# A fused recurrence and maxout layer: the start-up reordered, and one more block of input taken through the transposing DMA

## The chip, the cores and the metric

The kernel runs on one core of one Trainium2 chip. The metric is the device time in microseconds (us) of one execution; a time is quoted as the median of several executions, and the single ones are given where they scatter. The profile of a kernel is one of its executions, and its span is some 2 us shorter than the device time, because it runs only from the first to the last instruction.

The engines are called as the profile calls them: PE (matrix products), PEld (loading of PE's weights, which overlaps PE), DVE (vector work), ACT (activations), POOL and SP. In this kernel POOL does almost nothing but issue the DMAs that cast fp32 to bf16, and SP almost nothing but issue the other DMAs. All of them share the core's 16 DMA engines.

## The reference

A gated linear recurrence over 4 sequences of 6144 tokens with 256 features each, and a two-layer network on its result:

```python
sig = 1.0 / (1.0 + np.exp(-f_logit))
f = lower_bound + (1.0 - lower_bound) * sig
for t in range(S):                       # h: (B, D)
    h = f[:, t] * h + (1.0 - f[:, t]) * x[:, t]
    y[:, t] = h
# y: (24576, 256), w1 and w2: (256, 1024), w_out: (1024, 256)
g = np.maximum(y @ w1, y @ w2)
out = g @ w_out                          # (24576, 256) fp32
```

The kernel uses max(a, b) = a + relu(b - a). It needs only one first-layer product, with `wd` = w2 - w1, and adds `y @ w13`, with `w13` = w1 @ w_out, to the second layer.

## The kernel before: the parts that matter

Tokens are handled in blocks of 512. The first four blocks are chunks of their own; after them a chunk is 1024 tokens, two blocks. So "chunk 4" is blocks 4 and 5, "chunk 5" blocks 6 and 7, "chunk 6" blocks 8 and 9. For the recurrence, features must lie on the partitions and tokens along the free axis, so f and x must be transposed. There are two ways to do it:

```python
    def by_xbar(c, s):
        return c >= (4, 4)[s]            # chunks 0 to 3: PE transposes; from 4 on: DMA
    NSCR = 2
    scratch = [[dram.tile([CH, D], BF16, ...) for q in range(NSCR)] for s in range(2)]

    def fetch(c):                        # issued by POOL
        for s in range(2):               # s = 0: f, s = 1: x
            ...
            elif by_xbar(c, s):
                scr = scratch[s][uses[s] % NSCR]
                uses[s] += 1
                nc.gpsimd.dma_start(     # cast fp32 -> bf16, DRAM -> DRAM
                    out=scr[0:nt, :].rearrange("(p i) d -> p (i d)", p=P), in_=...)
                held[c, s] = scr
            else:
                ...                      # cast fp32 -> bf16, DRAM -> SBUF

    def cross(c):                        # issued by SP
        for s in range(2):
            if by_xbar(c, s):
                dst = inpool.tile([P, KC, CH], BF16, name=("fT", "xT")[s])
                nc.sync.dma_start_transpose(out=dst[:, :, 0:nt], in_=held[c, s][0:nt, :])
                held[c, s] = dst
```

There are two scratch buffers for f and two for x. The cast of a chunk into a scratch buffer must therefore wait until the transposing DMA of the chunk that used it last has read it. This wait follows from `uses[s] % NSCR`.

Per block: ACT makes u = sigmoid(-f) (`gate`), DVE makes v = u * x, the decay ff = 1 + nom * u, and the scan y. PE runs the first layer (`dT`), ACT evicts it through a relu (`rt`), PE runs the second layer of the block before (`psO`), DVE evicts that (`osb`) and SP issues its store. The main loop, cut:

```python
    LEAD_FETCH = 7
    LEAD_CROSS = 3
    ...                                  # blocks 0, 1, 2; weights; w13
        for j in range(2, NBLK + 1):
            ahead("cross", cross, j + LEAD_CROSS)
            ahead("fetch", fetch, j + LEAD_FETCH)
            ...
            if j == 2:
                for fc in range(FC):
                    second_layer(1, fc)
            for fc in range(FC):
                if j < NBLK:
                    first_layer(j, fc)
                if j > 2:
                    second_layer(j - 1, fc)
                ...
                if fc == 0 and j + 1 < NBLK:
                    scans = scan_steps(j + 1)
                if fc < len(scans):
                    scans[fc]()
```

Of the kernel before, what the change touches and what calls it, by code (L numbers as in the profile page):

```python
# [9 lines left out]
FP32 = mybir.dt.float32  # L10
BF16 = mybir.dt.bfloat16
# [7 lines left out]
def kernel(  # L19
# [36 lines left out]
    def by_xbar(c, s):  # L56
        return c >= (4, 4)[s]
# [33 lines left out]
    def fetch(c):  # L91
        b, t0, nt, _ = chunks[c]
        for s in range(2):
            src = srcs[s][b, t0 : t0 + nt, :]
            if c == 0:
                raw = const.tile([P, nt // P, D], FP32, name=("f0", "x0")[s])
                nc.sync.dma_start(  # L97
                    out=raw[:], in_=src.rearrange("(p i) d -> p i d", p=P)
                )
                nat = natpool.tile([P, CH // P, D], BF16, name=("fn", "xn")[s])  # L100
                nc.vector.tensor_copy(out=nat[:, 0 : nt // P, :], in_=raw[:])  # L101
                held[c, s] = nat
            elif by_xbar(c, s):
                scr = scratch[s][uses[s] % NSCR]
                uses[s] += 1
                nc.gpsimd.dma_start(  # L106
                    out=scr[0:nt, :].rearrange("(p i) d -> p (i d)", p=P),
                    in_=src.rearrange("(p i) d -> p (i d)", p=P),
                )
                held[c, s] = scr  # L110
            else:
                nat = natpool.tile([P, CH // P, D], BF16, name=("fn", "xn")[s])
                nc.gpsimd.dma_start(
                    out=nat[:, 0 : nt // P, :].rearrange(
                        "p (k i) d -> p k (i d)", i=TB // P
                    ),
                    in_=src.rearrange(
                        "(k p i) d -> p k (i d)", p=P, i=TB // P
                    ),
                )  # L120
                held[c, s] = nat

# [38 lines left out]
    def gate(j):  # L161
        nb = blocks[j][2]
        u = midpool.tile([P, KC, TB], BF16, name="u")
        src = turned[j, 0]
        nc.scalar.activation(  # L165
            out=like(u[:, :, 0:nb], src), in_=src, func=AF.Sigmoid, scale=-1.0
        )
        us[j] = u

    def like(t, src):  # L170
        if len(src.shape) == 3:
            return t
        return t.rearrange("p k (m i) -> p k m i", m=P)

    def scan_steps(j):
# [17 lines left out]
        def drive():  # L193
            src = turned[j, 1]
            nc.vector.tensor_tensor(  # L195
                out=like(v[:, :, 0:nb], src),
                in0=like(u[:, :, 0:nb], src),
                in1=src,
                op=ALU.mult,
            )  # L200

        def scan(h):
# [15 lines left out]
            drive,  # L218
            lambda: decay(0),
            lambda: decay(1),  # L220
            lambda: scan(0),
            lambda: scan(1),
        ]

# [42 lines left out]
    def pair(w, k):  # L267
        return w[:, :, 2 * k * P : 2 * k * P + 2 * P].rearrange(
            "p kc (q m) -> p kc q m", q=2
        )  # L270

    def make_wd(k):
        g, r = divmod(k, NQ // 2)
        qs = slice(2 * r, 2 * r + 2)
        nc.vector.tensor_tensor(  # L275
            out=pair(wdf, k), in0=half(w2n, g)[:, :, qs], in1=half(w1n, g)[:, :, qs],
            op=ALU.subtract,
        )
        cols = slice(2 * k * P, 2 * k * P + 2 * P)
        for kc in range(KC):  # L280
            nc.scalar.mul(wd[:, kc, cols], wdf[:, kc, cols], om[:, kc : kc + 1])  # L281
# [101 lines left out]
    with tc.manual_schedule():  # L383
# [6 lines left out]
        fetch(0)  # L390
        for g in range(NG):
            fetch_w(g)
        nc.scalar.activation(out=warm[:], in_=om[:, 0:1], func=AF.Sigmoid)
        wt = ps_d.tile([P, TB], BF16, name="dT")
        for q in range(8):
            nc.tensor.transpose(wt[:, 0:P], ident[:], ident[:])
        turn(turn_steps(0))
        recurrence(0)
        pool_waits(w1n[0][:, 0, 0:1])
        nc.gpsimd.dma_start(  # L400
            out=wob[:].rearrange("p (g q) c -> p g (q c)", g=NG),
            in_=moe_w_out.rearrange("(g p q) c -> p g (q c)", g=NG, q=NQ),
        )
        pool_waits(w2n[1][:, 0, 0:1])
        fetch(1)
        fetch(2)
        done["fetch"] = 3
        ahead("fetch", fetch, LEAD_FETCH)
        pts = [turn_w1(0), turn_w1(1)]
        make_wd(0)  # L410
        make_wd(1)
        for fc in range(0, 2):
            first_layer(0, fc)
        keep_w1T(0, pts[0])
        make_wd(2)
        for fc in range(2, 4):
            first_layer(0, fc)
        make_wd(3)
        keep_w1T(1, pts[1])
        pts = [turn_w1(2), turn_w1(3)]  # L420
        for fc in range(4, 6):
            first_layer(0, fc)
        keep_w1T(2, pts[0])
        for fc in range(6, 8):
            first_layer(0, fc)
        keep_w1T(3, pts[1])
        make_w13()
        turn(turn_steps(1))
        recurrence(1)
        for fc in range(FC):  # L430
            second_layer(0, fc)
# [6 lines left out]
        turn(turn_steps(3))  # L438
        gate(3)
        for j in range(2, NBLK + 1):  # L440
# [9 lines left out]
            if j == 2:  # L450
                for fc in range(FC):
                    second_layer(1, fc)
            for fc in range(FC):
# [8 lines left out]
                if fc == 0 and j + 1 < NBLK:  # L462
                    scans = scan_steps(j + 1)
# [32 lines left out]
```

## Time and profile before

| | before |
|---|---|
| time, median (3 executions) | 403.2 us (403.06 to 403.27) |
| span of the profile, granted PE clock | 401.1 us, 1.000 |
| PE busy | 386.0 us, 96% |
| first first-layer matmul | 13.47 us |
| first layer of block 3 starts in full | 41.48 us |
| from there, one block | 7.82 us |

The page of the kernel before, first and fourth part (busy us, share of the span, number of instructions; then the chain of work that ended last, by engine and by line):

```profile
PE 386.0 (96%) x2744; PEld 295.1 (74%) x2792; DVE 247.5 (62%) x349; ACT 269.5 (67%) x446; POOL 27.6 (7%) x59
...
PE 94%; DVE 3%; DMA 1%; issue 1%; SPq 0%; ACT 0%; DVEq 0%
```

A block's first layer starts "in full" with the second of the two matrix products that add up to its first piece; in block 3 the first of them ran at 40.31, on the half of y that was ready.

PE is the limit, and it is used nearly without a gap. The chain, in order of time, shows the last place where anything but PE is in it (start, length, what; all in us):

```profile
33.95 2.74 PE psO L346 x25
36.71 0.69 DVE osb L366
37.41 1.12 DVE v L195
38.53 0.53 DVE ff L184 x2
39.06 2.38 DVE y L208 x2
41.48 0.38 PE dT L317
```

Block 3's first layer at 41.48 waits for DVE, which did block 3's v, ff and scans only after two evictions. After it the chain is PE alone. What is to be won lies before 41.48.

The other thing to look at is DMA traffic. SP's DMA issues in the kernel before (start and length of the issuing instruction; when SP is long at a transposing DMA, the DMA engines are slow to take it):

```profile
28.83 8.36 SPq L128 DMA_TRANSPOSE fT<-scr_0_90  x1
37.30 3.05 SPq L128 DMA_TRANSPOSE xT<-scr_0_92  x1
40.44 0.53 SPq L369 DMA_DIRECT2D out_dram<-osb  x1
41.06 2.77 SPq L128 DMA_TRANSPOSE fT<-scr_1_91  x1
```

And POOL's cast issues (in brackets POOL's wait before them, and what ended it):

```profile
17.63 0.49 POOL L106 DMA_DIRECT2D scr_1_91<-in_f_logit_dram  x1 [0.73 <-DMA fn<-in_f_logit_dram]
18.87 0.49 POOL L106 DMA_DIRECT2D scr_1_93<-in_x_dram  x1 [0.75 <-DMA xn<-in_x_dram]
41.38 0.49 POOL L106 DMA_DIRECT2D scr_0_90<-in_f_logit_dram  x1 [22.02 <-DMA fT<-scr_0_90]
42.94 0.49 POOL L106 DMA_DIRECT2D scr_0_92<-in_x_dram  x1 [1.07 <-DMA xT<-scr_0_92]
```

The casts of chunks 4 and 5 are all issued by 18.87, with no wait for a transposing DMA, since both scratch buffers are fresh; counted from the trace, their last packet starts at 31.6 us and ends at 35.8. Chunk 4's transposing DMAs (blocks 4 and 5) are issued at 28.83 and 37.30 and have the DMA engines nearly to themselves from 36 to 42 us. The next casts come only at 41.38 and 42.94, when those have landed.

### The profile page before, as it was taken

How to read it: one execution, taken by the hardware profiler on the slowest of the kernel's cores; microseconds unless marked ns; L12 is line 12 of the kernel's file. 1: busy time of each engine (PE TensorE's matmuls, PEld its weight loads, DVE VectorE, ACT ScalarE, POOL GpSimd, SP SyncE). 2: the span in 40 equal slices, each digit the busy share in tenths (PEclk: the TensorE clock that was granted, in tenths of full speed). 3: DMA queues.
4: the chain of work that ended last, by engine and by line, in shares of the span. 5: the costliest groups of instructions: out<-in, count | busy, mean ns of one | idle time of the engine just before them, and what ended most of it. 6: DMA issues, size and time to landing. Idle time of an engine off the chain costs nothing.

```text
span 401.1 us, 6980 instructions
## 1 busy us (share of the span) xinstructions
PE 386.0 (96%) x2744; PEld 295.1 (74%) x2792; DVE 247.5 (62%) x349; ACT 269.5 (67%) x446; POOL 27.6 (7%) x59
## 2 busy tenths in 40 slices
PE   3899999999999999999999999999999999999996
PEld 2587677777777777777777777777777777777775
DVE  3866656656765665676567566656756665675641
ACT  2656676677667667766766776676667667666762
POOL 0700010010010000000000010000000000000000
PEclk9999999999999999999999999999999999999999
DMA  7999999799999799799899997997995998963212
GB/s 252 208 221 172 247 217 259 170 196 213 223 197 212 205 201 223 171 197 212 203 167 223 195 260 172 191 218 190 217 219 167 177 232 197 181 119 92 106 52 106
DMA packets 103088, 77.00 MB, mean 192 GB/s; under 512 B 93520, under 2 KB 94032, under 8 KB 102352
## 3 DMA queue, kind: packets, MB, share of 16 engines
q1 hardware_dynamic: 100224, 51.13, 52.1%
q0 software_dynamic: 2544, 25.17, 36.8%
q8 instruction: 22, 0.36, 0.4%
q10 hardware_dynamic: 288, 0.26, 0.2%
q14 instruction: 10, 0.08, 0.1%
HBM read 53.48 MB, written 48.23 MB: 254 GB/s over the span
## 4 chain that ended last, share of the span: by engine, by line
PE 94%; DVE 3%; DMA 1%; issue 1%; SPq 0%; ACT 0%; DVEq 0%
PE psO L346 54%; PE dT L317 39%; DMA x_124<-in_x_dram 1%; DVE y L208 1%; PE tT L155 1%; DVE v L195 1%; PE psO L301 0%; DVE ff L184 0%; DVE wdf L275 0%; PE psO L288 0%; DVE xn L101 0%; DVE osb L366 0%; ACT wd L281 0%; SPq L384 0%; SPq L97 0%
## 5 line engine op out<-in xcount | busy, mean ns | idle before, releaser
L325 ACT ACTIVATE rt<-dT 128x512 bf16<-128x512 f32 x384 | 222.1, 598 | 109.5 <-PE dT L317 109.4
L346 PE MATMUL psO<-wob,rt 128*128 128x256 bf16 x1536 | 228.5, 273 | 2.4
L317 PE MATMUL dT<-y,wd 128*128 128x512 bf16 x720 | 217.8, 382 | 2.4 <-ACT wd L281 1.4
L346 PEld LDWEIGHTS <-rt 128*128 128x128 bf16 x1536 | 169.8, 113 | 39.9
L366 DVE COPY osb<-psO 128x512 f32<-128x512 f32 x94 | 64.9, 691 | 75.4 <-PE psO L346 75.4
L208 DVE TENSOR_TENSOR_SCAN y<-ff,y,v 128x512 bf16<-128x512 bf16 x88 | 107.8, 1267 | 0.0
L317 PEld LDWEIGHTS <-wd 128*128 128x128 bf16 x768 | 75.1, 98 | 12.6 <-issue 2.7
L346 PE MATMUL psO<-w_109,y 128*128 128x256 bf16 x384 | 73.3, 273 | 0.0
L346 PEld LDWEIGHTS <-y 128*128 128x128 bf16 x384 | 43.1, 113 | 40.9 <-issue 1.1
L195 DVE TENSOR_TENSOR v<-u,xT 128x1024 bf16<-128x1024 bf16 x44 | 30.5, 692 | 61.2 <-ACT u L165 61.2
L165 ACT ACTIVATE u<-fT 128x1024 bf16<-128x1024 bf16 x44 | 46.2, 1050 | 0.0
L184 DVE TENSOR_SCALAR ff<-u,nom 128x512 bf16<-128x512 bf16 x96 | 29.2, 347 | 0.0
L106 POOL DMA_DIRECT2D scr_0_90<-in_f_logit_dram x11 | 5.4, 493 | 137.0 <-DMA fT<-scr_0_90 137.0
L106 POOL DMA_DIRECT2D scr_1_91<-in_f_logit_dram x11 | 5.5, 496 | 128.2 <-DMA fT<-scr_1_91 127.5
L208 DVE TENSOR_TENSOR_SCAN y<-ff,v 128x512 bf16<-128x512 bf16 x8 | 9.3, 1207 | 0.0
L165 ACT ACTIVATE u<-tT 128x1024 bf16<-128x1024 bf16 x4 | 4.2, 1049 | 7.5 <-PE tT L155 7.5
L195 DVE TENSOR_TENSOR v<-u,tT 128x1024 bf16<-128x1024 bf16 x4 | 4.9, 1218 | 5.4 <-ACT u L165 4.2
L281 ACT ACTIVATE wd<-wdf,om 128x256 bf16<-128x256 f32 x8 | 3.6, 502 | 5.4 <-DVE wdf L275 5.3
L106 POOL DMA_DIRECT2D scr_1_93<-in_x_dram x11 | 5.6, 511 | 16.1 <-DMA xT<-scr_1_93 15.3
L106 POOL DMA_DIRECT2D scr_0_92<-in_x_dram x11 | 5.4, 488 | 14.7 <-DMA xT<-scr_0_92 13.9
L155 PE MATMUL tT<-ident,fn 128*128 128x128 bf16 x32 | 2.9, 242 | 2.8 <-DVE fn L101 2.8
L155 PEld LDWEIGHTS <-fn 128*128 128x128 bf16 x32 | 2.4, 108 | 3.4 <-DVE fn L101 3.1
(34 smaller groups left out, 35.2 us busy)
## 6 DMA issues: line engine op xcount, KB each, us to landing
out_dram<-osb SPq DMA_DIRECT2D x47, 512.0 KB, 3.6
scr_0_90<-in_f_logit_dram POOLq DMA_DIRECT2D x11, 512.0 KB, 6.6
scr_0_92<-in_x_dram POOLq DMA_DIRECT2D x11, 512.0 KB, 8.4
scr_1_91<-in_f_logit_dram POOLq DMA_DIRECT2D x11, 512.0 KB, 6.5
scr_1_93<-in_x_dram POOLq DMA_DIRECT2D x11, 512.0 KB, 8.1
fn<-in_f_logit_dram POOLq DMA_DIRECT2D x3, 256.0 KB, 6.9
xn<-in_x_dram POOLq DMA_DIRECT2D x3, 256.0 KB, 7.6
f_120<-in_f_logit_dram SPq DMA_DIRECT2D x1, 512.0 KB, 3.5
```

Source lines behind the costliest of these rows:

```text
L106: nc.gpsimd.dma_start(out=scr[0:nt, :].rearrange("(p i) d -> p (i d)", p=P), in_=src.rearrange("(p i) d -> p (i d)", p=P),)
L155: nc.tensor.transpose(dst, src, ident[:])
L165: nc.scalar.activation(out=like(u[:, :, 0:nb], src), in_=src, func=AF.Sigmoid, scale=-1.0)
L184: nc.vector.tensor_scalar(out=ff[:, h, 0:nb], in0=u[:, h, 0:nb], scalar1=nom[:, h : h + 1], scalar2=1.0, op0=ALU.mult, op1=ALU.add,)
L195: nc.vector.tensor_tensor(out=like(v[:, :, 0:nb], src), in0=like(u[:, :, 0:nb], src), in1=src, op=ALU.mult,)
L208: nc.vector.tensor_tensor_scan(out=y[:, h, 0:nb], data0=ff[:, h, 0:nb], data1=v[:, h, 0:nb], initial=init, op0=ALU.mult, op1=ALU.add,)
L281: nc.scalar.mul(wd[:, kc, cols], wdf[:, kc, cols], om[:, kc : kc + 1])
L317: nc.tensor.matmul(dT[:, 0:nb], lhsT=wd[:, kc, fc * P : (fc + 1) * P], rhs=y[:, kc, 0:nb], start=(kc == 0), stop=(kc == KC - 1),)
L325: nc.scalar.activation(out=rt[:, 0:nb], in_=dT[:, 0:nb], func=AF.Relu)
L346: nc.tensor.matmul(ps[:, r, :], lhsT=left, rhs=right, start=(s == 0 and (r == 0 or j == NBLK - 1)), stop=(s == n - 1 and (r == 1 or j == N ...
L366: nc.vector.tensor_copy(out=osb[:, 2 * g : 2 * g + 2, :], in_=ps[:])
```

## The change

Its intent is to shorten the head, the time before PE runs without a gap, by five means: block 0's recurrence in two halves, so that it starts after half of the load; the first weight difference in pieces of 128 columns, so that the first matmul comes sooner; the cast of w_out issued as soon as the first w2 half has landed; the transposing DMAs of chunks 3 and 4 queued ahead of the stores; and block 3 taken through the transposing DMA in place of PE. In passing, ff is computed before v, and block 3's scans are put into block 1's second layer. The diff, cut to its core:

```diff
     def by_xbar(c, s):
-        return c >= (4, 4)[s]
+        return c >= 3
@@ fetch: the case c == 0 goes; two half loads by SP instead
+    def fetch_first(k):
+        nt = TB // 2
+        for s in range(2):
+            raw = const.tile([P, nt // P, D], FP32, name=f"raw{k}{s}")
+            nc.sync.dma_start(out=raw[:], in_=srcs[s][0, k * nt : (k + 1) * nt, :]...)
+    ...                     # first_bf16, first_turn, first_recurrence(k): half k of block 0
@@ scan_steps
         return [
-            drive,
             lambda: decay(0),
             lambda: decay(1),
+            drive,
             lambda: scan(0),
             lambda: scan(1),
         ]
@@ weight difference: pieces of n * 128 columns; second half scaled by DVE, not ACT
-    def make_wd(k):
+    def make_wd(fc, n):
...
+            if g == 0:
+                nc.scalar.mul(wd[:, kc, cols], wdf[:, kc, cols], om[:, kc : kc + 1])
+            else:
+                nc.vector.tensor_scalar_mul(...)
@@ start
-        fetch(0)
+        fetch_first(0)
+        fetch_first(1)
         for g in range(NG):
             fetch_w(g)
+        pool_waits(w2n[0][:, 0, 0:1])
+        nc.gpsimd.dma_start(out=wob[:]..., in_=moe_w_out...)
+        done["fetch"] = done["cross"] = 1
+        ahead("fetch", fetch, 4)                 # chunks 1 to 4
...
-        pool_waits(w1n[0][:, 0, 0:1])
-        nc.gpsimd.dma_start(out=wob[:]..., in_=moe_w_out...)
-        pool_waits(w2n[1][:, 0, 0:1])
-        fetch(1)
-        fetch(2)
-        done["fetch"] = 3
-        ahead("fetch", fetch, LEAD_FETCH)        # chunks 3 to 5
...
         turn(turn_steps(1))
         recurrence(1)
+        ahead("cross", cross, 4)                 # chunks 3 and 4, before block 0's store
         for fc in range(FC):
             second_layer(0, fc)
@@ main loop
             if j == 2:
+                if 0 in gates:
+                    gate(gates.pop(0))
+                early = scan_steps(j + 1)
                 for fc in range(FC):
                     second_layer(1, fc)
+                    if fc < 4:
+                        early[fc]()
+                early[4]()
...
-                if fc == 0 and j + 1 < NBLK:
+                if fc == 0 and 2 < j < NBLK - 1:
                     scans = scan_steps(j + 1)
```

Chunk 3 now takes the first scratch buffer of each pair, chunk 4 the second, and chunk 5 the first again. Before, chunk 4 took the first and chunk 5 the second.

More of the change, by code (lines that the diff above doesn't have):

```diff
@@ L94, in fetch @@
             src = srcs[s][b, t0 : t0 + nt, :]
-            if c == 0:
-                raw = const.tile([P, nt // P, D], FP32, name=("f0", "x0")[s])
-                nc.sync.dma_start(
-                    out=raw[:], in_=src.rearrange("(p i) d -> p i d", p=P)
-                )
-                nat = natpool.tile([P, CH // P, D], BF16, name=("fn", "xn")[s])
-                nc.vector.tensor_copy(out=nat[:, 0 : nt // P, :], in_=raw[:])
-                held[c, s] = nat
-            elif by_xbar(c, s):
+            if by_xbar(c, s):
                 scr = scratch[s][uses[s] % NSCR]
@@ L121, in fetch, with first_bf16, first_turn @@
                 held[c, s] = nat
+    raws = {}
+    def fetch_first(k):
+        nt = TB // 2
+        for s in range(2):
+            raw = const.tile([P, nt // P, D], FP32, name=f"raw{k}{s}")
+            nc.sync.dma_start(
+                out=raw[:],
+                in_=srcs[s][0, k * nt : (k + 1) * nt, :].rearrange(
+                    "(p i) d -> p i d", p=P
+                ),
+            )
+            raws[k, s] = raw
+    def first_bf16(k, s, copy):
+        raw = raws[k, s]
+        nat = const.tile([P, raw.shape[1], D], BF16, name=f"nat{k}{s}")
+        copy(out=nat[:], in_=raw[:])
+        raws[k, s] = nat
+    def first_turn(k):
+        nt = TB // 2
+        for s in range(2):
+            dst = ps_t.tile([P, KC, nt // P, P], BF16, name="tT")
+            for q in range(nt // P):
+                for h in range(KC):
+                    nc.tensor.transpose(
+                        dst[:, h, q, :],
+                        raws[k, s][:, q, h * P : (h + 1) * P],
+                        ident[:],
+                    )
+            raws[k, s] = dst[:].rearrange("p k i m -> p k m i")
     def cross(c):
@@ L163, in gate @@
         u = midpool.tile([P, KC, TB], BF16, name="u")
-        src = turned[j, 0]
+        fT = turned[j, 0]
         nc.scalar.activation(
-            out=like(u[:, :, 0:nb], src), in_=src, func=AF.Sigmoid, scale=-1.0
+            out=like(u[:, :, 0:nb], fT), in_=fT, func=AF.Sigmoid, scale=-1.0
         )
@@ L193, in drive @@
         def drive():
-            src = turned[j, 1]
+            xT = turned[j, 1]
             nc.vector.tensor_tensor(
-                out=like(v[:, :, 0:nb], src),
-                in0=like(u[:, :, 0:nb], src),
-                in1=src,
+                out=like(v[:, :, 0:nb], xT),
+                in0=like(u[:, :, 0:nb], xT),
+                in1=xT,
                 op=ALU.mult,
@@ L223, in scan_steps, with first_recurrence @@
         ]
+    first = {}
+    def first_recurrence(k):
+        nt = TB // 2
+        cols = slice(k * nt, (k + 1) * nt)
+        if k == 0:
+            for t in ("u", "ff", "v"):
+                first[t] = midpool.tile([P, KC, TB], BF16, name=t)
+            ys[0] = ypool.tile([P, KC, TB], BF16, name="y")
+        u, ff, v, y = (*(first[t] for t in ("u", "ff", "v")), ys[0])
+        fT, xT = raws[k, 0], raws[k, 1]
+        nc.scalar.activation(
+            out=like(u[:, :, cols], fT), in_=fT, func=AF.Sigmoid, scale=-1.0
+        )
+        for h in range(KC):
+            nc.vector.tensor_scalar(
+                out=ff[:, h, cols],
+                in0=u[:, h, cols],
+                scalar1=nom[:, h : h + 1],
+                scalar2=1.0,
+                op0=ALU.mult,
+                op1=ALU.add,
+            )
+        nc.vector.tensor_tensor(
+            out=like(v[:, :, cols], xT), in0=like(u[:, :, cols], xT), in1=xT,
+            op=ALU.mult,
+        )
+        for h in range(KC):
+            nc.vector.tensor_tensor_scan(
+                out=y[:, h, cols],
+                data0=ff[:, h, cols],
+                data1=v[:, h, cols],
+                initial=y[:, h, nt - 1 : nt] if k else 0.0,
+                op0=ALU.mult,
+                op1=ALU.add,
+            )
     def recurrence(j):
@@ L265, in pool_waits @@
         nc.gpsimd.tensor_copy(out=waited[:], in_=t)
-    def pair(w, k):
-        return w[:, :, 2 * k * P : 2 * k * P + 2 * P].rearrange(
-            "p kc (q m) -> p kc q m", q=2
-        )
-    def make_wd(k):
-        g, r = divmod(k, NQ // 2)
-        qs = slice(2 * r, 2 * r + 2)
+    def make_wd(fc, n):
+        g, r = divmod(fc, NQ)
+        qs = slice(r, r + n)
+        cols = slice(fc * P, (fc + n) * P)
         nc.vector.tensor_tensor(
-            out=pair(wdf, k), in0=half(w2n, g)[:, :, qs], in1=half(w1n, g)[:, :, qs],
+            out=wdf[:, :, cols].rearrange("p kc (q m) -> p kc q m", q=n),
+            in0=half(w2n, g)[:, :, qs],
+            in1=half(w1n, g)[:, :, qs],
             op=ALU.subtract,
         )
-        cols = slice(2 * k * P, 2 * k * P + 2 * P)
         for kc in range(KC):
-            nc.scalar.mul(wd[:, kc, cols], wdf[:, kc, cols], om[:, kc : kc + 1])
+            if g == 0:
+                nc.scalar.mul(wd[:, kc, cols], wdf[:, kc, cols], om[:, kc : kc + 1])
+            else:
+                nc.vector.tensor_scalar_mul(
+                    out=wd[:, kc, cols], in0=wdf[:, kc, cols], scalar1=om[:, kc : kc + 1]
+                )
     def turn_w1(k):
@@ L389 @@
         nc.vector.tensor_scalar_add(out=nom[:], in0=lbc[:], scalar1=-1.0)
-        fetch(0)
+        fetch_first(0)
+        fetch_first(1)
         for g in range(NG):
             fetch_w(g)
+        pool_waits(w2n[0][:, 0, 0:1])
+        nc.gpsimd.dma_start(
+            out=wob[:].rearrange("p (g q) c -> p g (q c)", g=NG),
+            in_=moe_w_out.rearrange("(g p q) c -> p g (q c)", g=NG, q=NQ),
+        )
+        done["fetch"] = done["cross"] = 1
+        ahead("fetch", fetch, 4)
         nc.scalar.activation(out=warm[:], in_=om[:, 0:1], func=AF.Sigmoid)
@@ L396 @@
             nc.tensor.transpose(wt[:, 0:P], ident[:], ident[:])
-        turn(turn_steps(0))
-        recurrence(0)
-        pool_waits(w1n[0][:, 0, 0:1])
-        nc.gpsimd.dma_start(
-            out=wob[:].rearrange("p (g q) c -> p g (q c)", g=NG),
-            in_=moe_w_out.rearrange("(g p q) c -> p g (q c)", g=NG, q=NQ),
-        )
-        pool_waits(w2n[1][:, 0, 0:1])
-        fetch(1)
-        fetch(2)
-        done["fetch"] = 3
-        ahead("fetch", fetch, LEAD_FETCH)
+        first_bf16(0, 0, nc.vector.tensor_copy)
+        first_bf16(0, 1, nc.vector.tensor_copy)
+        first_turn(0)
+        first_recurrence(0)
+        first_bf16(1, 0, nc.scalar.copy)
+        first_bf16(1, 1, nc.scalar.copy)
+        first_turn(1)
+        first_recurrence(1)
+        for fc in range(2):
+            make_wd(fc, 1)
+        make_wd(2, 2)
         pts = [turn_w1(0), turn_w1(1)]
-        make_wd(0)
-        make_wd(1)
-        for fc in range(0, 2):
+        for fc in range(2):
             first_layer(0, fc)
-        keep_w1T(0, pts[0])
-        make_wd(2)
+        for k in range(2):
+            keep_w1T(k, pts[k])
         for fc in range(2, 4):
             first_layer(0, fc)
-        make_wd(3)
-        keep_w1T(1, pts[1])
+        make_wd(4, 2)
+        make_wd(6, 2)
         pts = [turn_w1(2), turn_w1(3)]
-        for fc in range(4, 6):
+        for fc in range(4, 8):
             first_layer(0, fc)
-        keep_w1T(2, pts[0])
-        for fc in range(6, 8):
-            first_layer(0, fc)
-        keep_w1T(3, pts[1])
+        for k in range(2):
+            keep_w1T(2 + k, pts[k])
         make_w13()
@@ L437 @@
             step()
-        turn(turn_steps(3))
-        gate(3)
+        steps = turn_steps(3)
+        turn(steps)
+        if steps:
+            gate(3)
         for j in range(2, NBLK + 1):
```

## The prediction

This was written before the changed kernel had been run.

> **What bounds the kernel now.** TensorE. The page gives PE 96% busy of a 401.1 us span at granted clock 1.0, and the chain that ended last is 94% PE. In that chain, from 41.48 us on, a block costs 7.82 us and no gap is left: 45 such blocks, 4.4 us of last second layer and some 3.3 us of last eviction and store end the span. None of this changes, so what can be won lies before 41.48 us, the start of block 3's first layer.
>
> **That head, from the timeline and the chain.** f and x land at 4.75 and 6.0; DVE runs v 1.22, ff 0.6, scans 2.33, and y(0) is ready at 11.9; the weight difference (1.05 for 256 columns) and its scaling (0.5) put the first first-layer matmul at 13.47. The first 8 take 3.60 instead of 1.7 us: one every 0.43 us, later every 0.217. The Trainium skill ("TensorE: Matmul & The Clock Gate", Part 1) describes a half-rate clock until the array has been busy some 3.4 us; the trace agrees. w13 ends at 21.5, block 1's first layer starts at 27.5 (ACT-bound, 3.94), block 3's transposes take 0.9, and before 41.48 PE waits about 1.1 for block 3's v, ff and scans, which start only at 37.3.
>
> **What the change does (estimates from those durations).**
> 1. Halves: first half of f lands about 4.1; y(0) complete about 10.3. First weight piece 0.55 + 0.3, so the first first-layer matmul comes at about 12.1, right behind the w1 transposes (10.1 to 12.05): gain 1.3 to 1.6. PE is then dense from 10.1 and may reach full rate earlier (0 to 1.5 more).
> 2. Second-half scaling moves from ACT to DVE, about neutral; w13 ends about 19.9.
> 3. Earlier w_out cast: starts near 9.5 and shares DMA with the second weight halves, which land about 13.8 instead of 12.6, just when DVE wants them. No gain, small risk.
> 4. Block 3 by transposing DMA: removes 16 of 64 input transposes (0.9). Its v reads SBUF (0.69, not 1.22), and its scans move into block 1's second layer: the 1.1 us wait goes.
>
> Sum: block 3's first layer starts at about 38 instead of 41.5.
>
> **What takes some back.** DMA. In the trace, block 4's transposes, issued at 28.8, show hardly any packets until the cast queue drains at 32; they land at 41.4 (f) and 42.9 (x), and y(4) is done at 48.4, only 0.9 before it is needed. The Trainium skill ("DMA: Bandwidth & Descriptors", Queues, rings and completion order) says that each engine alternates between queues by packet; cast packets here are 32 KB, transposing ones under 512 B. The changed kernel needs block 4 some 3.4 us sooner, with another chunk transposed ahead of it; transposes ahead of stores buy part of that. I expect block 4's x at 40.5 to 42.5 and a wait of 0 to 1.5 us at block 4.
>
> **Prediction.** 399.8 us, 80% range 398.0 to 401.9. Faster by over 2% 0.03, within 2% 0.95, slower by over 2% 0.02.
>
> **What would show each step.** First first-layer matmul at 12.1 +- 0.5; w13's end near 19.9; no PE transposes for block 3; its first layer at 37.5 to 38.8 without a wait for scans; then 7.82 per block, apart from one wait at block 4, released by a transposing DMA; a head shorter by 2.5 to 4 us, an unchanged tail.
>
> **What would make it wrong.** Second weight halves landing past 15 (w13 late, gain gone); block 3's transposes landing past 33 (ACT holds up evictions, PE stalls twice); block 4 landing past 43; or the clock rising early, with no stall: 398.

## The result, and the profile after

The changed kernel is slower. Its four executions took 416.55, 414.49, 448.63 and 415.46 us, the median being 416.0; the one of 448.63 counts as slow and is left out of the comparison. Against four executions of the kernel before in the same rounds (median 403.24) the ratio is 1.030, 95% interval 1.027 to 1.034. Here and below a ratio is the mean time of one kernel's fast executions over the mean of the other's in the same rounds, so it is not quite the ratio of the medians. The profile was taken in a fast execution.

| | before | after |
|---|---|---|
| span of the profile, granted clock | 401.1, 1.000 | 414.8, 0.981 |
| first first-layer matmul | 13.47 | 12.34 |
| w13 done, block 1's transposes start | 21.33 | 19.67 |
| block 1's first layer starts | 27.48 | 25.82 |
| block 3's first layer starts in full | 41.48 | 37.99 |
| block 4's first layer starts in full | about 49.3 (41.48 + 7.82) | 60.06 |

Up to block 3 the change does what it was meant to do: block 3's first layer begins 3.5 us sooner. Then 14 us are lost at block 4. The waits of the kernel after between 14 and 70 us (who waits for whom: us in total, times, longest):

```profile
ACT rt L389 <- PE dT L381: 22.6, 13, 14.2
POOL scr_0_90 L98 <- DMA fT<-scr_0_90: 19.9, 2, 13.1
...
DVE v L220 <- DMA xT<-scr_1_93: 13.9, 1, 13.9
PE dT L381 <- DVE y L233: 13.1, 2, 12.5
```

Read from below: PE waits for block 4's y, y's chain waits at v, and v waits 13.9 us for one transposing DMA, block 4's x. The chain of the kernel after says the same:

```profile
30.74 25.59 DMA xT<-scr_1_93
...
56.35 0.69 DVE v L220
57.05 0.60 DVE osb L430
57.65 2.38 DVE y L233 x2
...
60.06 0.59 PE dT L381
```

That transfer was issued at 30.74 and landed 25.59 us later. Before, block 4's x took 5.1 us from issue to landing. SP's issues in the kernel after:

```profile
22.48 1.31 SPq L153 DMA_TRANSPOSE fT<-scr_0_90  x1
23.90 4.60 SPq L153 DMA_TRANSPOSE xT<-scr_0_92  x1
28.59 2.06 SPq L153 DMA_TRANSPOSE fT<-scr_1_91  x1
30.74 7.50 SPq L153 DMA_TRANSPOSE xT<-scr_1_93  x1
38.33 4.21 SPq L433 DMA_DIRECT2D out_dram<-osb  x2
42.64 16.30 SPq L153 DMA_TRANSPOSE fT<-scr_0_90  x1
```

The first two are chunk 3, the next two chunk 4, the last is chunk 5. And POOL's casts:

```profile
30.14 0.49 POOL L98 DMA_DIRECT2D scr_0_90<-in_f_logit_dram  x1 [13.10 <-DMA fT<-scr_0_90]
31.39 0.61 POOL L98 DMA_DIRECT2D scr_0_92<-in_x_dram  x1 [0.76 <-DMA xT<-scr_0_92]
41.15 0.49 POOL L98 DMA_DIRECT2D scr_1_91<-in_f_logit_dram  x1 [9.15 <-DMA fT<-scr_1_91]
```

Chunk 5's casts, which before had a fresh buffer, are held 13.1 us for chunk 3's transposing DMA and let go at 30.14 and 31.39, just as block 4's x is issued (30.74). A third cast follows at 41.15. So block 4's x has three casts and two stores beside it. The table of stretches shows what became of DMA and PE (stretch; length; busy us of each engine; granted PE clock; mean busy share of the DMA engines, where overlapping packets count twice; GB/s). First the kernel before, then the kernel after:

```profile
40.00:50.00 10.00, 9.17 (x64) 6.67 (x64) 6.40 (x9) 6.93 (x13) 0.97 (x2) 1.00 1.08 248
```

```profile
40.00:50.00 10.00, 5.86 (x41) 4.21 (x40) 0.62 (x2) 4.79 (x8) 0.49 (x1) 1.00 1.28 94
50.00:60.00 10.00, 0.61 (x1) 0.13 (x2) 3.65 (x5) 0.00 (x0) 0.49 (x1) 0.56 0.74 152
60.00:70.00 10.00, 9.88 (x55) 6.64 (x56) 4.87 (x8) 5.42 (x9) 0.97 (x2) 0.76 1.28 273
```

Between 40 and 50 us the share of the DMA engines is higher than before (1.28 against 1.08), and they move less than half, 94 GB/s against 248. Packets are in flight all the time; but a share above 1 counts packets that wait as well as packets that move, so it does not say how much the engines work. PE stands still, its clock is throttled (0.56, then 0.76), and block 4 starts at half rate: a first-layer pair takes 0.85 us instead of 0.43.

The account closes. Block 4 could have started at 37.99 + 7.82 = 45.8 and started in full at 60.06, 14.3 us later. The half rate costs 2.3 us: the single first-layer product that the chain of before shows 4.83 us after block 3's start (46.31) comes 7.15 us after block 4's start here (67.21). The head gave 3.5. So -3.5 + 14.3 + 2.3 = +13.1 us, and that is what lies between the starts of the last second layer, 392.78 before and 405.86 after; so in between a block takes the same time again. The spans differ by 13.7; the other 0.6 us is in the last eviction and store.

### The profile page after: what moved, and what is told of

Same layout as the page of the kernel before. It is cut to its first block, busy times and chain, and to the rows that moved or that the text cites. A ratio compares the mean times of both kernels' runs of the same rounds, so it can differ in the third digit from the quotient of the medians.

```text
span 414.8 us, 6944 instructions
## 1 busy us (share of the span) xinstructions
PE 387.3 (93%) x2728; PEld 294.7 (71%) x2776; DVE 248.4 (60%) x359; ACT 269.7 (65%) x447; POOL 26.5 (6%) x58
## 4 chain that ended last, share of the span: by engine, by line
PE 84%; DMA 10%; SPq 2%; DVE 1%; POOL 1%; issue 1%
PE psO L410 49%; PE dT L381 35%; DMA xT<-scr_1_93 6%; DMA scr_0_90<-in_f_logit_dram 2%; SPq L153 2%; DMA w2n_112<-in_moe_w_dram 1%; DVE y L233 1%; SPq L121 0%; POOL fn L105 0%; POOL xn L105 0%; POOL wob L459 0%; DVE v L220 0%; DVE osb L430 0%; SPq L448 0%; DVE osb L419 0%
## 5 line engine op out<-in xcount | busy, mean ns | idle before, releaser
L381 PE MATMUL dT<-y,wd 128*128 128x512 bf16 x720 | 218.1, 382 | 14.0 <-DVE y L233 13.1
L190 ACT ACTIVATE u<-fT 128x1024 bf16<-128x1024 bf16 x45 | 47.4, 1053 | 1.5 <-DMA fT<-scr_1_91 1.5
L220 DVE TENSOR_TENSOR v<-u,xT 128x1024 bf16<-128x1024 bf16 x45 | 30.8, 685 | 13.9 <-DMA xT<-scr_1_93 13.9
L233 DVE TENSOR_TENSOR_SCAN y<-ff,v 128x512 bf16<-128x512 bf16 x6 | 7.0, 1208 | 0.0
L190 ACT ACTIVATE u<-tT 128x1024 bf16<-128x1024 bf16 x2 | 2.0, 1023 | 4.3 <-PE tT L180 4.3
L352 PE MATMUL psO<-ident_f,w1n_110 128*128 128x128 f32 x8 | 2.0, 422 | 2.8 <-DMA w1n_110<-in_moe_w_dram 2.8
L341 ACT ACTIVATE wd<-wdf,om 128x128 bf16<-128x128 f32 (+1 forms) x6 | 2.2, 427 | 3.7 <-DVE wdf L333 3.7
L352 PEld LDWEIGHTS psO<-ident_f,w1n_110 128*128 128x128 f32 x8 | 1.6, 221 | 3.1 <-issue 3.1
(49 smaller groups left out, 42.5 us busy)
```

What stands on the lines that cost most here:

```text
L190: nc.scalar.activation(out=like(u[:, :, 0:nb], fT), in_=fT, func=AF.Sigmoid, scale=-1.0)
L220: nc.vector.tensor_tensor(out=like(v[:, :, 0:nb], xT), in0=like(u[:, :, 0:nb], xT), in1=xT, op=ALU.mult,)
L233: nc.vector.tensor_tensor_scan(out=y[:, h, 0:nb], data0=ff[:, h, 0:nb], data1=v[:, h, 0:nb], initial=init, op0=ALU.mult, op1=ALU.add,)
L341: nc.scalar.mul(wd[:, kc, cols], wdf[:, kc, cols], om[:, kc : kc + 1])
L352: nc.tensor.transpose(pt[:, kc, q, :], half(w1n, g)[:, kc, 2 * r + q], ident_f[:])
L381: nc.tensor.matmul(dT[:, 0:nb], lhsT=wd[:, kc, fc * P : (fc + 1) * P], rhs=y[:, kc, 0:nb], start=(kc == 0), stop=(kc == KC - 1),)
```

## The experiments

Theories:

- A: chunk 5's casts, released by chunk 3's use of the scratch buffers, run beside block 4's transposing DMAs, and that starves them. A sub-form of it says that it is the long packets of the casts (32 KB each in the trace, 2.43 us alone) that do it.
- B: there is simply too much to move before block 4 is needed; whatever the order, it cannot be ready.
- C: the order of transposing DMAs against stores is at fault, since the stores now come behind or between them.
- D: something in the reordered head is at fault.

All kernels below gave correct results, except the microbenchmark. The kernel before was run beside them on the same chip and was never slow there (402.62 to 404.17 us).

### Block 3 back on PE, the rest kept (a1)

```diff
     def by_xbar(c, s):
-        return c >= 3
+        return c >= 4
```

> The changed kernel with block 3 transposed by TensorE again (one number: the transposing DMA starts with the chunk of blocks 4 and 5); all else as changed. Then the casts of blocks 6 and 7 need no scratch buffer that a transpose must free, so they are issued at about 18 us and drain before the first transpose, as in the kernel before. Theory A (casts released while transposes are in flight bring the DMA engines to a crawl) and theory B (the whole set of early transfers is simply too much for the DMA) both expect the collapse to go: block 4's x lands at 41 to 44 us, 400 to 402.5 us. Theory C (the collapse comes from the four transposes put ahead of the first stores) expects the two remaining early transposes still to hurt: over 405 us. Theory D (the halves of block 0 or the earlier w_out cast are at fault) expects over 410 us.

Measured: 435.73, 435.77, 401.07 and 434.48 us. One execution is what was expected, three are not. In the profile, which is one of the 435 us ones, there is no single stall at block 4; the whole run is slow, with SP mostly 7 to 12 us at a transposing DMA. The three are executions of the slow state, so this run neither confirms nor refutes A for the 416 us; what they show is told below ("a mode of its own"). The fast one, 401.07, is what A and B had expected, but it has no profile. A third pair of scratch buffers, which would have let chunk 5's casts go as early as before, was not tried.

### Shorter packets for the casts (a2)

```diff
-                    out=scr[0:nt, :].rearrange("(p i) d -> p (i d)", p=P),
-                    in_=src.rearrange("(p i) d -> p (i d)", p=P),
+                    out=scr[0:nt, :].rearrange("(k p i) d -> p k (i d)", k=2, p=P),
+                    in_=src.rearrange("(k p i) d -> p k (i d)", k=2, p=P),
```

> The changed kernel with the casts to scratch cut so that each row of a packet is 2 to 4 KB instead of one 32 KB piece per engine; order, bytes and waits as changed. Theory A in its packet form (a 32 KB cast packet holds an engine for 2.4 us and more, and a transpose, whose packets are under 512 B[...], stands still while any one engine holds one) expects no collapse: block 4's x lands before 42 us, 398.5 to 401 us. Theory B (too many bytes) expects no change: 413 to 418 us. Theory C (order against the stores) expects no change.

Measured: 409.56, 422.05 (slow), 414.65 (slow) and 406.93 us, ratio of the two fast ones 1.012 (1.007 to 1.017). The cast packets are now 2 KB (0.173 us each) and not 32 KB, and v still waits 8.7 us for block 4's x. The collision is milder and does not go away. So A's packet form, which had expected no collapse, missed: packet length is at most part of the size.

### Chunk 5's casts held until block 4's x has landed (a3)

```diff
             if j == 2:
+                pool_waits(held[4, 1][:, 0, 0:1])
```

The line stands ahead of the fetch of chunk 5. `pool_waits` makes POOL read one element of a tile, so this only adds a wait; nothing else is moved or taken away.

> The changed kernel with one wait more: GpSimd issues the casts of blocks 6 and 7 only once block 4's x transpose has landed, so no cast runs beside the first four transposes. Packets stay at 32 KB. Theory A expects block 4's x at 34 to 37 us instead of 56, no wait at block 4, and 398.5 to 400.5 us. Theory B expects little: the same bytes, later; over 408 us. Theory C expects no change, 413 to 418 us.

Measured: 401.58, 400.34, 400.86 and 399.93 us, ratio 0.993 (0.9905 to 0.9954). POOL's and then SP's issues in this kernel:

```profile
38.30 0.18 POOL L327 CAST waited<-xT 128x1 f32<-128x1 bf16 x1 [19.39 <-DMA xT<-scr]
38.83 0.49 POOL L98 DMA_DIRECT2D scr<-in_f_logit_dram  x1 [0.35 <-issue]
```

```profile
32.78 2.18 SPq L153 DMA_TRANSPOSE xT<-scr  x1
35.05 2.07 SPq L433 DMA_DIRECT2D out_dram<-osb  x2
```

Block 4's x, issued at 32.78, has landed at about 38.2, in 5.4 us (A had expected 34 to 37 us, so it came a little late); the casts go out after it. No stall is left and PE is busy 10.00 of 10 us in every stretch from 30 to 70. The same bytes pass through the same engines, and 15 us come back by adding a wait. This confirms A and refutes B and, as a cause of the 416 us, D. C is not needed to explain it: the stores were left where they were.

### One store ahead of chunk 4's transposing DMAs (a4)

```diff
-        ahead("cross", cross, 4)
+        ahead("cross", cross, 3)
```

> The changed kernel with only block 3's two transposes ahead of the first store; those of blocks 4 and 5 come behind the store of block 0, as in the kernel before. Theory A expects the collapse to stay, since the casts of blocks 6 and 7 are still released by block 3's transposes and run beside those of block 4: 408 to 420 us. Theory C (the order against the stores is the cause) expects under 403 us.

Measured: 404.06, 408.31 (slow), 400.85 and 401.93 us, ratio of the fast ones 0.997 (0.993 to 1.001). A's expectation, 408 to 420, missed; C's, under 403, holds for two of the three fast ones. In the profile the collision is still there: chunk 5's casts are issued at 32.72 and 33.87, block 4's transposing DMAs at 32.03 and 35.15, and block 4's x takes 11.0 us to land. But it does not take 25.6, and v waits only 1.2 us for it. So the order against the stores matters for the size. That it does so by shifting the transfers against one another is argued, not shown.

### Transposing DMAs alone and beside other transfers (b1)

This kernel computes nothing that is wanted. It issues four transposing DMAs of 512 KB, in stages, alone and beside four other transfers of 512 KB each, with a wait for everything between the stages:

```python
        for q in range(N):                       # stage 2: alone
            turn(q)
        barrier(xT)
        for q in range(N):                       # stage 3: beside casts to DRAM
            turn(q)
            cast(q, dst_scr)
        barrier(xT, dst_scr)
        ...                                      # casts to SBUF, fp32 stores, fp32 loads
```

> A kernel that computes nothing (its result is wrong on purpose) and measures the transfers of this case by themselves, in seven stages parted by barriers, four transfers of each kind per stage, 512 KB each on the bf16 or store side: 1 casts to DRAM alone; 2 transposes alone; 3 transposes and casts to DRAM issued together; 4 transposes and casts to SBUF (2 KB packets) together; 5 transposes and fp32 stores together; 6 transposes and fp32 loads together; 7 casts and stores, no transpose. From the traces: four casts alone about 10 to 11 us, four transposes alone about 10 us. If the engines only shared (theory B: too many bytes), stage 3 takes about the sum, 20 to 22 us. If a transpose beside a cast brings the engines to a crawl (theory A), stage 3 takes 30 us or more, as the trace of the changed kernel suggests, in which 30.7 to 56 us moved one transpose, three casts and part of two stores. If only long packets do it, stage 4 is about the sum of its parts; the run with short packets speaks against that, so I expect stage 4 to be slow too. Stages 5 and 6 tell whether any other transfer does it; I expect them near the sum (12 to 17 us), and stage 7 at the sum.

SP's issues in it (stages 2 to 5: alone, beside casts to DRAM, beside casts to SBUF, beside stores):

```profile
16.97 8.80 SPq L66 DMA_TRANSPOSE xT<-src_scr  x4
...
28.64 23.89 SPq L66 DMA_TRANSPOSE xT<-src_scr  x4
...
60.20 19.48 SPq L66 DMA_TRANSPOSE xT<-src_scr  x4
...
82.66 13.27 SPq L66 DMA_TRANSPOSE xT<-src_scr  x4
```

From the first issue until all had landed it took 11.1 us alone, about 26.5 beside casts to DRAM (I had expected 30 or more if A holds, 20 to 22 if B does), 21.6 beside casts to SBUF, 16.0 beside stores and 21.7 beside loads (for both I had expected 12 to 17). The four casts to DRAM alone took 12.6, so beside them the stage takes some 3 us more than the sum. Casts to SBUF beside stores, without a transposing DMA, took 18.6.

For casts to DRAM the share of the DMA queues, times the length of the window, gives the time of the packets, averaged over the 16 engines: casts alone 64.6% of 16 us, 10.3 us; transposing alone 87.8% of 11.8 us, 10.4 us. Together, in a window of 31.3 us, the casts take 34.3%, 10.7 us, and the transposing DMAs 51.9%, 16.2 us. So beside casts to DRAM the times of the same transposing packets add up to 56% more. The excess is not spread over them: half take 0.018 us or less in both stages, and 46 of the 8192, of 0.5 to 2.5 us each, make up nearly all of it. With casts to SBUF the stage takes no more than the sum (21.6 us, against 11.1 + 12.6 if a cast to SBUF is taken as long as one to DRAM, which is an estimate from the above).

Counted from the packets of the trace: while the casts to DRAM run (30.0 to 46.4 us), 1270 of the 8192 transposing packets of 256 bytes start, most of them in two bursts at 33 and 41 us; alone, at some 890 per us (8192 in 9.2 us), that is the work of 1.4 us. The others come through only when the casts are done. With the 2 KB casts to SBUF, 276 transposing packets start beside 260 of the casts between 66 and 69 us, nearly one for one. That agrees with the Trainium skill ("DMA: Bandwidth & Descriptors", Queues, rings and completion order), which says that an engine serves its queues by turns, a packet at a time.

Turns alone do not explain the casts to DRAM. From 42.3 to 46.3 us one cast packet at a time is in flight, so it can be on one of the 16 engines only; yet in these 4 us just 32 transposing packets start, and some 19 that have started stay in flight about as long as the cast packet. In this execution a single cast packet of 32 KB was enough to hold a transposing DMA on all engines. Why, no run shows.

### The head alone: block 3 on PE and no early transposing DMAs (b2)

```diff
     def by_xbar(c, s):
-        return c >= 3
+        return c >= 4
@@
-        ahead("cross", cross, 4)
```

> The changed kernel's head alone: first block in halves, finer first weight pieces, w_out cast sooner; block 3 by TensorE and the first transposes back in their old place, behind the store of block 0. Worth of the head by the trace of the changed kernel: its block 1 starts about 1.65 us sooner than before, so 401 to 402.5 us. Theory A expects no collapse, but the pattern of casts and transposes is as near to one as in the run with block 3 on TensorE, so a slow run of some 430 us would not surprise it; theory C (transposes ahead of stores) expects no slow run at all.

Measured: 400.9, 401.82, 400.9 and 400.84 us, ratio 0.994 (0.992 to 0.997), slightly better than expected. In its chain block 3's first layer starts at about 39.2, behind PE work alone, without a wait for DVE. So of the roughly 3 us to be had, the reordered head gives nearly all; block 3 through the transposing DMA and the early transposing DMAs add what a3 has over b2 (see d1 and d2), a few tenths, and bring the trouble. D is refuted a second time. And a1 differs from b2 only in the early transposing DMAs, chunk 4 ahead of the stores: with that line three executions of four were slow, without it none of four.

### The w_out cast back behind the first w1 half, with a3's wait (b3)

```diff
-        pool_waits(w2n[0][:, 0, 0:1])
+        pool_waits(w1n[0][:, 0, 0:1])
@@
             if j == 2:
+                pool_waits(held[4, 1][:, 0, 0:1])
```

> The changed kernel with the casts of blocks 6 and 7 held (as in the run that held them), and the w_out cast put back behind the first half of w1. If the sooner cast takes DMA time from the weights, the first w1 piece lands up to 0.5 us sooner and the time falls to 399.5 to 400.3 us; if it is neutral, as predicted, 400.3 to 401.

Measured: 432.17, 400.13, 399.88 and 400.79 us; the ratio of the fast ones is 0.992 (0.990 to 0.994), not to be told from a3 (the fast median, 400.1, lies in the range given for a cast that takes time from the weights, but the two kernels' executions overlap). The sooner cast of w_out is worth nothing measurable. The first execution, which is the profiled one, was slow as in a1.

### Every pair of casts held until both f and x of the chunk that had its buffers have landed (b4)

```diff
+                if s == 0 and c >= 5:
+                    pool_waits(held[c - 2, 1][:, 0, 0:1])
```

> The changed kernel in which every pair of casts to scratch from block 6 on waits for the x transpose of the chunk whose scratch it fills, not only for its own f or x transpose. Theory A expects what the first hold gave or a little less, 399.5 to 401 us, with less spread, because no cast is ever released while the second transpose of a pair is in flight. Theory B expects a loss, since each f cast starts some 2 us later: over 403 us.

Measured: 406.04, 427.07 (slow), 410.56 (slow) and 403.01 us, ratio of the two fast ones 1.003 (0.997 to 1.008). A's expectation missed, and the number lies in B's range. The rule holds chunk 5's casts for chunk 3's x, which landed at 30.4, and block 4's x was issued at 30.25: so they were let go into the same collision, and v still waits 5.6 us for block 4's x. The trace agrees with A's mechanism; the expectation had overlooked that the rule names the wrong chunk.

### A mode of its own: casts before transposing DMAs, by rule (c1, c2)

The profiles of the slow executions (435.73 us in a1, 432.17 in b3) show another picture than the stall at block 4. Nothing of the 416 us rests on them, and what makes them slow is not shown; they are described here because the next two experiments start from them. SP's and POOL's issues in a1:

```profile
76.72 9.98 SPq L153 DMA_TRANSPOSE fT<-scr  x1
86.78 7.84 SPq L153 DMA_TRANSPOSE xT<-scr  x1
...
95.81 9.93 SPq L153 DMA_TRANSPOSE fT<-scr  x1
```

```profile
76.35 0.49 POOL L98 DMA_DIRECT2D scr<-in_f_logit_dram  x1 [17.48 <-DMA fT<-scr]
79.64 0.49 POOL L98 DMA_DIRECT2D scr<-in_x_dram  x1 [2.80 <-DMA xT<-scr]
95.48 0.49 POOL L98 DMA_DIRECT2D scr<-in_f_logit_dram  x1 [15.36 <-DMA fT<-scr]
```

In this stretch each chunk's first cast is released within half a microsecond of the issue of the next chunk's transposing DMAs (76.35 and 76.72; 95.48 and 95.81). The period is some 19 us, where PE needs 15.64 for a chunk (twice 7.82). I had the idea that the collision keeps itself up, because SP no longer pauses at the stores. SP's waits for finished outputs before a store, in the kernel before, in a1 and in c1 (below):

```profile
SPq L369 <- DVE osb L366: 231.4, 44, 24.0
```

```profile
SPq L433 <- DVE osb L430: 31.1, 6, 7.4
```

```profile
SPq L437 <- DVE osb L434: 29.5, 5, 7.4
```

In the kernel before SP arrives at most stores before the output is ready and waits for it, 231 us in all (210 in b2); in a1 it waits 31. But the wait does not mark the slow state: c1, whose executions are all fast, has 29.5 (its SP waits at the added loads instead), and in a1 SP waits 132 us for ACT before its transposing DMAs instead (39 in the kernel before). So the idea is not shown.

To test it, c1 (on b3) and c2 (on a1) make SP read one row of the next chunk's scratch before it issues a chunk's transposing DMAs, so that those always come after the casts:

```diff
+        if 5 <= c < NCHUNK - 1:
+            for s in range(2):
+                nc.sync.dma_start(out=probe[:], in_=held[c + 1, s][0:1, :])
```

> The kernel with the held casts and the later w_out cast (399.9 to 400.8 us, but 432 once in four), and one rule more: from block 6 on, the sync engine issues a chunk's transposes only when the casts of the next chunk have landed, which a load of one row from their scratch makes it wait for. Casts and transposes then hardly share the engines at all. If the slow executions are a collision that keeps itself up (each transpose that lands late releases casts just as the next transpose is issued, because the stores that used to part them are by then ready and hold nothing back), there is none left: six executions of 399.5 to 401 us, none over 405. By the transfers measured alone, a chunk's two casts take about 5 us, its transposes 4.4 and its two stores 2.6, 12 of the 15.6 us that TensorE takes for it; with latencies the chain fits only just, so if the waits themselves cost too much every execution comes out some us slower, 403 to 410. If the slow executions have another cause, they stay.

Measured for c1, six executions: 406.76 to 410.47 us, ratio 1.012 (1.009 to 1.015), none near 432, about the range given for waits that cost too much (403 to 410).

> The kernel with block 3 on TensorE, which took 434 to 436 us in three of four executions and 401.07 in one, with the same rule: transposes from block 6 on only after the casts of the next chunk have landed. If the collision keeps itself up, all four executions take 400.5 to 402.5 us. If the 434 us come from anything else (the chip, the order of the first transposes and stores, which is left as it was), executions over 420 us stay.

Measured for c2: 410.01, 413.32, 408.85 and 408.12 us, ratio 1.016 (1.012 to 1.021). The 434s are gone, and so is the 401; the expected 400.5 to 402.5 was missed. SP's issues in c1:

```profile
67.98 2.13 SPq L156 DMA_TRANSPOSE fT<-scr  x1
70.15 2.20 SPq L156 DMA_TRANSPOSE xT<-scr  x1
...
81.70 1.99 SPq L152 DMA_DIRECT2D probe<-scr  x2
83.74 1.85 SPq L156 DMA_TRANSPOSE fT<-scr  x1
```

Kept apart from the casts, each transposing DMA takes SP only about 2 us; in the fast profile of a3 those of f take 7 to 9. What makes the slow state is not shown by this: b3 was slow once in four executions, so six of c1 without it prove little, and a1 and b3 ran on another chip than c1 and c2. The cost of the rule is clear, though: the loop of cast, landing, transposing DMA, landing now has a period of 16.2 us (seven periods between the first lines of chunks at 52.15 and 165.42 us), above PE's 15.64, so the rule itself becomes the limit.

### The two best kernels again, five rounds on the same chip (d1 = a3, d2 = b2)

> The kernel of a3 once more, only for the spread of its executions. If the collision mode near 432 us is a matter of chance that a3's rule for one pair of casts does not exclude, as its near twin b3 suggests, one or more of these executions may show it; the fast ones should lie at 399.9 to 401.6 again, ratio 0.991 to 0.995. If all are fast, twice over, the mode is rarer in this form than one in eight.

Measured: 400.05 to 400.86 us, median 400.35, ratio 0.9925 (0.991 to 0.994).

> The kernel of b2 once more. Its early chunks are not transposed ahead of the stores, so in its trace the sync engine waits 210 us for finished outputs, as before the change (231), against 31 in the two profiled slow executions. If that pacing is what keeps the collision mode away, all executions lie at 400.8 to 401.9, ratio 0.992 to 0.997, and none near 432.

Measured: 400.59 to 401.0 us, median 400.81, ratio 0.9935 (0.992 to 0.995). SP's waits for outputs were 186.1 us in d1's profile and 226.7 in d2's. With the earlier runs each kernel has nine executions, all fast. Both beat the kernel before by 0.6 to 0.8%. The 0.3 to 0.5 us by which a3 leads (the executions of d1 and d2 overlap) is what block 3 through the transposing DMA and the early transposing DMAs are worth when nothing goes wrong. That b3, nearly the same kernel as a3, was slow once in four executions makes b2 the more careful choice; nine clean executions of each do not prove that a3 is exposed to it, nor that b2 is not.

## Why the prediction was wrong

- **PE as the limit, 7.82 us a block, an unchanged tail: right.** After 65 us both kernels run alike, but for 0.6 us in the last eviction and store.
- **The head: right.** Predicted: first first-layer matmul at 12.1 (measured 12.34), w13 done at 19.9 (block 1's transposes begin at 19.67), block 3's first layer at about 38 (37.99) without a wait for scans. The half-rate start fits the Trainium skill ("TensorE: Matmul & The Clock Gate", Part 1), which has the array throttled until it has been busy for a few us: the first 8 matmuls took 3.60 us before and 2.53 after. By the spacing of the matmuls the full rate came 3.4 us after the first first-layer matmul before, 3.0 us after PE's w1 transposes began in the kernel after, and some 4.8 us after block 4's start there. b2 shows that this head alone gives 0.6%.
- **"Earlier w_out cast ... No gain, small risk": no gain, right** (b3's fast executions and a3's cannot be told apart).
- **The step that failed: "I expect block 4's x at 40.5 to 42.5 and a wait of 0 to 1.5 us at block 4."** It landed at 56.3, v waited 13.9 us, and PE, 14.3 us late, lost another 2.3 us at half rate. The prediction did name DMA as the danger and "block 4 landing past 43" as what would make it wrong, and even the sharing by packets. But it costed block 4's transposing DMAs from the trace of before, where chunk 5's casts had been issued by 18.87 and drained before. It did not ask what releases those casts after the change. By adding chunk 3 to the users of the two scratch buffers, the change tied chunk 5's casts to the landing of chunk 3's transposing DMAs, at 30.14, the very time at which block 4's x was issued (30.74). So the overlap was mistaken, not only its price. a3 takes only this coincidence away and gets 400.6 us, inside the range predicted, so the rest of the sum held.
- **The size.** A sum of the parts would not have been enough either. With the durations of b1 alone (2.8 us a transposing DMA, 2.6 a cast, 1.2 a store: 11.1 / 4, 10.3 / 4, (16.0 - 11.1) / 4), block 4's x, three casts, two stores and part of block 6's f make about 14 us (an estimate); the window was 25.6.

Open: why the engines do so much worse than the sum. In the kernel after, a transposing packet that starts while block 4's x is under way (30.7 to 56.35 us) takes 0.056 us on the mean, where alone in b1 it is 0.020. The median is 0.018 in both; 80 packets of 3558 take over 0.5 us and make up most of the difference. What holds them is not shown by any run, nor why the same two casts beside block 4's x cost 11.0 us until it landed in a4 and 25.6 here. Also open is what decides, in one execution and not in another, whether the slow state comes.

## What to carry to other kernels

When a change adds a user to a rotating buffer, follow the release: list what the later landing lets go, and look what that will run beside. A transfer costed from a trace in which it ran alone has no known cost when something else is released into it. A transposing DMA whose result is waited for is best kept off the time of casts: a single wait, on the queue that has slack, was worth 15 us here. Keeping the two apart everywhere was not: c1 and c2 lost 1.2 to 1.6% against the kernel before. And run several executions before trusting a reordered DMA queue: one of 401 us stood beside three of 435.

## What the Trainium skill lacked or had wrong

- "DMA: Bandwidth & Descriptors", Rules for kernel authors, says that a transpose next to ordinary DMAs "needs nothing". It speaks of wrong results there, and the results were right in every kernel that computes them; but it does not hold for time: four transposing DMAs took 11.1 us alone, about 26.5 beside casts from DRAM to DRAM, 21.6 beside casts to SBUF and 16.0 beside stores.
- The same page, SWDGE vs HWDGE vs iDMA, gives a packet as preferably at most 4096 bytes. The casts to DRAM here run in what the profile counts as packets of 32 KB, 2.43 us each alone (the median in b1) and up to 7.47 us in the kernel after.
- The same page, Queues, rings and completion order, has service by turns at packet granularity, and the trace agrees (276 packets of the one to 260 of the other in 3 us). It lacks that a transposing DMA can stand still on all engines for one packet on one of them: 32 of its packets started in 4.0 us of b1 while a single 32 KB cast packet at a time was in flight, where alone some 890 start in one.
- The same page, Issuing engines are not separate DMA queues, says that all DMAs interleave on the same 16 engines. It does not say that sharing can cost more than the sum: in b1 transposing DMAs and casts to DRAM took about 26.5 us together, and 11.1 and 12.6 alone.
- No page tells of a program on one core whose executions fall into two groups so far apart: 401 against 435 us for a1, 400 against 432 for b3. What decides is open.
